# A conv, SiLU and ELU kernel on one core: block scales fetched and set earlier, taps moved between units, the last sums in one bank

## Chip, core and metric

One NeuronCore of a Trainium2 chip. The time is the device time of one execution in microseconds, the median of the runs shown. TensorE (PE; its weight loads are PEld), VectorE (DVE), ScalarE (ACT), GpSimd (POOL) and SyncE (SP, which issues most of the transfers) each work through a queue of their own in order.

## What is computed

```python
w = softmax(weight)                              # 8 heads x 7 taps
x = causal 7-tap convolution of x with w         # 8192 tokens x 192
h = x @ w_in;  x = (h * sigmoid(h)) @ w_out      # layer 0, SiLU, d_ff 2048
h = x @ w_in2; out = elu(h) @ w_out2             # layer 1, ELU, d_ff 2048
```

All in float32 accuracy. The kernel splits each factor into a high and a low part and multiplies high by high, high by low and low by high. From block 3 of layer 0 on, the low part of the activation g is float16, and to fit it is scaled by a power of two, one per block.

## The kernel before

The tokens stand in 16 blocks of 512, and a layer takes a block in 8 units, one for each eighth of d_ff (256 of 2048). Units are numbered in the order in which they run: blocks 0 and 1 of layer 0 share units 0 to 15, and block b from 2 on has units 8b to 8b+7, the first of which is called s. Layer 1 follows from unit 128.

From unit 20 on TensorE's queue holds for unit n: the in-products of n (18 matmuls, line 546, into a PSUM tile `h` with two buffers), then the out-products of an earlier unit. For blocks from 3 on these are the high products of unit n-3 (line 646), and after those of unit 8b+10 also the low products of block b: `low_c` (line 658) and `low_ab` (line 670), whose weights `w16` and activations `lo` are float16, in 64 x 64 tiles. So after block 5's low ab sums come the in-products of unit 51.

For unit n of a scaled block in layer 0, ScalarE makes SiLU in place in `h` (line 588) and the high part `g_hi` (line 580, scaled by `forth`), and VectorE the low part `lo` (line 583). `lo` is the last reader of `h`, so the in-products of unit n wait for `lo` of unit n-2.

Everything else is filled in by hand. `at(step, f, part)` notes f for a unit, and `run_fill(step)` issues what is noted for it ahead of that unit's SiLU, `g_hi` and `lo` on each queue (where a block ends, parts 1 and 2 go behind them). For the next block b this is, in order:

- the convolution: 14 taps on VectorE (line 499, 501), for the 128 rows of group 0 (512 tokens) and the folded 64 rows of group 1 in turn;
- `measure`: VectorE finds the largest magnitude of each row, and SP sends it to a small table in memory (`shared<-sum`, line 417, the share);
- `split_conv`: ScalarE and VectorE split the rows into high and low parts, and SP issues four crossings (`x_hl<-x_hl`, line 314) that bring each half of the rows to the other 64 partitions. Unit s reads crossed rows from its third pair of products on;
- `fetch`: SP brings the whole table to all partitions (`all<-shared`, line 421). It must wait for the share to land. The tile `all` has one buffer, for both layers' blocks and for the weights' bounds;
- `set_scale`: VectorE sums the table and makes `forth` and `back` (six small operations, lines 450 to 458).

In blocks 8 to 15 VectorE and ScalarE also make one eighth of layer 1's weights: the halves of `val` (lines 141, 145, 149) in units s-3 and s-2, then in unit s-1 three copies on ScalarE (lines 363, 211, 363). Layer 1's weight bound is measured up to unit 53, shared in 54, fetched by POOL in 56 and worked out by `finish_weight_scale(1)` in unit 58 (lines 473 to 443); unit 61 is the first to need it.

At the end `last_ab` sums the low ab products of the last block for two halves of 256 tokens. It has two PSUM banks for each half, one for the upper and one for the lower 64 rows of the contraction, and `add_ab` adds both to the output, one after the other, ahead of the store.

Of the kernel before, what the change touches and what calls it, by code (L numbers as in the profile page):

```python
# [9 lines left out]
F32 = mybir.dt.float32  # L10
# [14 lines left out]
P = 128  # L25
HP = 64
TB = 512
HT = TB // 2
# [10 lines left out]
NEW = 3  # L39
# [6 lines left out]
def kernel(  # L46
# [34 lines left out]
    ps_h = ctx.enter_context(tc.tile_pool(name="ps_h", bufs=2, space=bass.MemoryType.PSUM))  # L81
# [7 lines left out]
    ROWS = slice(0, HP), slice(HP, P)  # L89
# [219 lines left out]
    def load_x(b, *groups):  # L309
        for f in x_loads(b, *groups):  # L310
            f()
# [61 lines left out]
    def keep_ab(b, y):  # L373
        kept["ab", b] = tc.dram_tile([P, TB], F32, name="kept_ab")
        nc.sync.dma_start(out=kept["ab", b], in_=y)
# [25 lines left out]
    w16_t = {}  # L401
# [4 lines left out]
    def scaled(layer, b):  # L406
        return layer == 1 or b >= NEW

    def small(n=1, dtype=F32, tag=None):
        return scale_p.tile([P, n], dtype, tag=tag or f"small{n}", name=tag or "small")  # L410
# [8 lines left out]
    def fetch(key, queue=nc.sync):  # L419
        t = fixed.tile([P, 2 * P], F32, tag="all", name="all")  # L420
        queue.dma_start(out=t, in_=shared[key].to_broadcast([P, 2 * P]))
        shared[key] = t

    def measure(layer, b, *of):
        t = stat[layer, b] = small(2, tag="sum")
        for k, x in enumerate(of):
            nc.vector.tensor_reduce(
                out=t if len(of) == 1 else t[:, k : k + 1], in_=x, axis=AX.X, op=ALU.max, apply_absolute_value=True
            )
        share((layer, b), t)  # L430

    def power(out, of, exponent):

        nc.vector.tensor_scalar(
            out=of.bitcast(I32), in0=of.bitcast(I32), scalar1=EXP, scalar2=None, op0=ALU.bitwise_and
        )
        nc.vector.tensor_scalar(
            out=out.bitcast(I32), in0=of.bitcast(I32), scalar1=-1.0, scalar2=float((254 + exponent - 1) << 23),
            op0=ALU.mult, op1=ALU.add,
        )  # L440

    def inverse(out, of):
        nc.vector.tensor_scalar(
            out=out.bitcast(I32), in0=of.bitcast(I32), scalar1=-1.0, scalar2=float(254 << 23),
            op0=ALU.mult, op1=ALU.add,
        )

    def set_scale(layer, b):
        total = small(tag="total")
        nc.vector.tensor_reduce(out=total, in_=shared[layer, b], axis=AX.X, op=ALU.add)  # L450
        nc.vector.tensor_scalar(
            out=total, in0=total, scalar1=most[layer][:, 0:1], scalar2=TINY, op0=ALU.mult, op1=ALU.max
        )
        s = forth[layer, b] = small(tag="forth")
        power(s, total, 26)
        r = back[layer, b] = small(tag="back")
        inverse(r, s)
        nc.vector.tensor_tensor(out=r, in0=r, in1=down[layer], op=ALU.mult)
# [12 lines left out]
    def finish_weight_scale(layer):  # L471
        m = most[layer] = fixed.tile([P, 2], F32, tag=f"most{layer}", name="most")
        nc.vector.tensor_reduce(
            out=m, in_=shared[layer].rearrange("p (n two) -> p two n", two=2), axis=AX.X, op=ALU.max
        )
        largest = small(tag="total")
        nc.vector.tensor_scalar_max(largest, most[layer][:, 1:2], TINY)
        up[layer] = fixed.tile([P, 1], F32, tag=f"up{layer}", name="up")
        down[layer] = fixed.tile([P, 1], F32, tag=f"down{layer}", name="down")
        power(up[layer], largest, 14)  # L480
        inverse(down[layer], up[layer])
# [42 lines left out]
    g_t = {}  # L524
    g_of = {}
    acc_t = {}
# [133 lines left out]
                    rhs=g_t[u][1][ROWS[r], i, :], start=False, stop=last,  # L660
                )

    def low_ab(u, last, banks=None, tokens=slice(0, TB), first=False):

        layer, b, q = u
        for i in range(2):
            for j in range(2):
                for r in range(2):
                    bank = acc_t[layer, b, f"ab{r}"] if banks is None else banks[:, r, :]
                    nc.tensor.matmul(  # L670
                        out=bank[ROWS[j], :], lhsT=w16_t[layer, q][ROWS[r], i, ts(j, HP)],
                        rhs=g_t[u][1][ROWS[r], i, tokens], start=first and i == 0, stop=last and i == 1,
                    )

    def low_products(layer, b):
        us = [(layer, b, q) for q in range(NQ)]
        for u in us:
            low_c(u, u == us[-1])
        for u in us:
            low_ab(u, u == us[-1])  # L680

    def last_ab(tokens):

        bank = ps_h.tile([P, 2, TB], F32, tag="h", name="last")[:, :, 0:HT]
        for u in units[-NQ:]:
            low_ab(u, u == units[-1], bank, tokens, u == units[-NQ])
        return bank
# [67 lines left out]
    def end_steps(layer, b):  # L755

        both = xin.tile([P, TB], F32, tag="conv1", name="both")
        if layer == 0:
            y = mid.tile([P, TB], F32, tag="ab", name="mid_ab")
        else:  # L760
            y = xin.tile([P, TB], F32, tag="conv0", name="o")

        def plus(to, of):
            if scaled(layer, b):
                nc.vector.scalar_tensor_tensor(
                    out=to, in0=of, scalar=back[layer, b], in1=to, op0=ALU.mult, op1=ALU.add
                )
            else:
                nc.vector.tensor_add(out=to, in0=of, in1=to)

        def add(name, to):
            halves = [acc_t.pop((layer, b, f"{name}{r}")) for r in range(2)]
            scale = back[layer, b] if scaled(layer, b) else 1.0
            nc.scalar.activation(out=to, in_=halves[0], func=ACTF.Copy, scale=scale)  # L774
            plus(to, halves[1])

        def store_ab(cols=slice(0, TB)):
            nc.sync.dma_start(out=outT[0:P, b * TB + cols.start : b * TB + cols.stop], in_=y[:, cols])

        def add_ab(banks=()):  # L780
            if not banks:
                add("ab", y)
                if layer == 0:
                    keep_ab(b, y)
                elif b < NB - 1:
                    store_ab()
                return
            tokens, bank = banks
            for r in range(2):
                plus(y[:, tokens], bank[:, r, :])  # L790
            store_ab(tokens)

        return both, lambda: add("c", both), add_ab
# [24 lines left out]
    def at(step, f, part=0):  # L818
        fill.setdefault((max(step, 0), part), []).append(f)
# [5 lines left out]
    def spread(steps, first, n):  # L825
        for k, f in enumerate(steps):
            at(first + k * n // len(steps), f)
# [20 lines left out]
    for b in range(2, NB):  # L848
        s = where[0, b, 0]
        if b > 2:  # L850
            at(s - 14, lambda b=b: pending.extend(x_loads(b)) if b < 5 else load_x(b))
        steps = [f for fs in zip(*(conv_steps(b, g) for g in range(2))) for f in fs]
        found_it = [lambda b=b: measure(0, b, conv_t[b, 0], conv_t[b, 1])]
        splits = [lambda b=b, g=g: split_conv(b, g) for g in range(2)]
        if b <= 3:
            spread(steps + found_it * (b == NEW) + splits, s - 10, 7 if b > 2 else 8)
        elif b == 4:
            spread(steps, s - 10, 7)
            at(s - 4, found_it[0])
        else:  # L860
            for k, f in enumerate(steps):
                step = s - 8 if k < 1 else s - 7 if k < 2 else s - 6
                at(step, f, 0 if k < 5 else 1 if k < 10 else 2)
            at(s - 5, found_it[0])
        if b >= 4:
            for f in splits:
                at(s - 4 + (b == 4), f)
        if b >= NEW:
            at(s - 3 + (b == 4), lambda b=b: fetch((0, b)))
            at(s - 1, lambda b=b: set_scale(0, b))  # L870
    for b in range(NB):
        at(where[1, b, 0] - 9, lambda b=b: load_mid(b))
        at(where[1, b, 0] - 6, lambda b=b: split_mid(b), 1)
# [15 lines left out]
    look = where[0, 6, 6]  # L889
    at(look, lambda: set_weight_scale(1, found))  # L890
    at(look + 2, lambda: fetch(1, nc.gpsimd))
    at(look + 4, lambda: finish_weight_scale(1), 2)
    made = {}
    for k, q in enumerate([*range(1, NQ), 0]):
        s = where[0, 8 + k, 0]
# [9 lines left out]
    with tc.manual_schedule():  # L905
# [3 lines left out]
        for _ in range(9):  # L909
            nc.tensor.matmul(  # L910
                out=warm, lhsT=ones, rhs=ones.unsqueeze(1).to_broadcast([P, TB // P, P]), start=True, stop=True
# [82 lines left out]
        for rows, other, _ in PAIRS:  # L994
# [9 lines left out]
            out=conv_ps, in0=x_raw[1][:, 0, TAPS - 1 : TAPS - 1 + TB], scalar=tap_w[:, 0, TAPS - 1 : TAPS],  # L1004
# [80 lines left out]
        for s in range(4, TWO + 3):  # L1085
# [5 lines left out]
            q = s // 2 + 1  # L1091
# [24 lines left out]
        for s in range(TWO + 4, n_units):  # L1116
            u = units[s]
# [38 lines left out]
        banks = [(tokens, last_ab(tokens)) for tokens in HALF]  # L1156
# [49 lines left out]
```

## Time and profile before

| | |
|---|---|
| median of 3 runs | 1077.77 us (1077.63 to 1078.63) |
| the profiled execution | 1078.69 us, its span 1077.0 us |
| TensorE busy | 1068.6 us, 99% of the span |
| its weight loads | 840.8 us, 78% |
| VectorE, ScalarE | 820.3 us, 76%, and 813.4 us, 76% |
| GpSimd | 89.3 us, 8% |
| granted TensorE clock | 1.0 throughout |

The span runs from the first to the last instruction; all times of rows count from its start. A row of the timeline gives start, duration, engine, line, operation, output<-inputs, form and count, and in brackets how long the engine was idle before it and what ended that.

### The profile page before, as it was taken

Reading aid. Unit: us, or ns where it says so; the run is one execution under the profiler, and the core shown is the slowest. Engines: PE = TensorE matmul, PEld = TensorE weight load, DVE = VectorE, ACT = ScalarE, POOL = GpSimd, SP = SyncE. Lnnn points to the kernel's source line nnn. Section 1 sums busy time; section 2 is a strip of 40 time slices with the busy share of each in tenths; the row PEclk is TensorE's granted clock in tenths of the full one; section 3 lists DMA queues with packets and bytes.
Section 4 is the critical chain, followed back from the end, with each engine's and each line's share of the span. In section 5 each row is a group of like instructions: output and inputs, shape, how many; then the busy total and the mean of one; then the engine's idle time right before and its main releaser. Section 6 shows DMA issues by size and latency. Waiting matters only on the chain.

```text
span 1077.0 us, 25189 instructions
## 1 busy us (share of the span) xinstructions
PE 1068.6 (99%) x10755; PEld 840.8 (78%) x10755; DVE 820.3 (76%) x1125; ACT 813.4 (76%) x907; POOL 89.3 (8%) x139
## 2 busy tenths in 40 slices
PE   9999999999999999999999999999999999999998
PEld 6999978777777777787777787777777777877776
DVE  8998767777777888777567777778777777777766
ACT  7767766556677666676688988888988888888885
POOL 5521131000110011100200000000000000000000
PEclk9999999999999999999999999999999999999999
DMA  5413165323443332323541122212123210222200
GB/s 162 134 46 85 30 168 145 101 68 80 116 113 80 109 107 92 109 79 85 161 139 46 26 60 60 60 38 40 44 60 60 59 37 26 60 60 60 40 16 16
DMA packets 48768, 82.77 MB, mean 77 GB/s; under 512 B 10576, under 2 KB 22736, under 8 KB 48656
## 3 DMA queue, kind: packets, MB, share of 16 engines
q1 hardware_dynamic: 42416, 57.30, 21.5%
q0 software_dynamic: 6240, 23.86, 7.5%
q8 instruction: 84, 1.38, 0.6%
q14 instruction: 28, 0.23, 0.1%
HBM read 43.23 MB, written 18.12 MB: 57 GB/s over the span
## 4 chain that ended last, share of the span: by engine, by line
PE 94%; DVE 2%; DMA 2%; SPq 1%; issue 1%; ACT 1%; DVEq 0%
PE h L546 46%; PE ab L646 19%; PE c L646 9%; PE ab L670 9%; PE c L658 5%; PE ab L719 2%; PE c L719 1%; PE ab L627 1%; DMA x_hl<-x_hl 1%; DVE conv L501 1%; PE c L627 1%; SPq L314 0%; DMA all<-shared 0%; DVE lo L583 0%; DMA raw<-in_w_dram 0%
## 5 line engine op out<-in xcount | busy, mean ns | idle before, releaser
L546 PE MATMUL h<-x_hl,wi 64*128 64x512 f32 x4464 | 573.4, 388 | 3.2 <-DVE lo L583 2.3
L546 PEld LDWEIGHTS h<-x_hl,wi 64*128 64x128 f32 x4464 | 435.2, 184 | 96.9 <-issue 7.0
L592 DVE SCALAR_TENSOR_TENSOR g<-g,h 128x1024 f32<-128x1024 f32 x128 | 156.3, 1221 | 129.1 <-ACT g L591 129.1
L646 PE MATMUL ab<-g_hi,wo 64*128 64x512 f32 x1856 | 248.1, 386 | 0.0
L646 PEld LDWEIGHTS ab<-g_hi,wo 64*128 64x128 f32 x1856 | 173.9, 184 | 36.5
L583 DVE SCALAR_TENSOR_TENSOR lo<-h,forth,g_hi 128x1024 f16<-128x1024 f32 x104 | 133.4, 1282 | 83.8 <-ACT g_hi L580 83.7
L588 ACT ACTIVATE h<-h 128x1024 f32<-128x1024 f32 x104 | 104.8, 1008 | 92.8 <-PE h L546 90.6
L583 DVE SCALAR_TENSOR_TENSOR lo<-g,forth,g_hi 128x1024 f16<-128x1024 f32 x128 | 163.6, 1278 | 0.1
L590 ACT ACTIVATE g<-h 128x1024 f32<-128x1024 f32 x128 | 131.6, 1029 | 42.4 <-PE h L546 42.4
L580 ACT ACTIVATE g_hi<-g,forth 128x1024 fp32r<-128x1024 f32 x126 | 143.2, 1136 | 0.0
L646 PE MATMUL c<-g_hi,wo 64*128 64x512 f32 x928 | 143.0, 386 | 0.0
L591 ACT ACTIVATE g<-g 128x1024 f32<-128x1024 f32 x128 | 135.7, 1060 | 4.0
L580 ACT ACTIVATE g_hi<-h,forth 128x1024 fp32r<-128x1024 f32 x104 | 116.1, 1116 | 3.4
L670 PE MATMUL ab<-lo,w 64*64 64x512 f16 x1792 | 101.5, 376 | 0.0
L646 PEld LDWEIGHTS c<-g_hi,wo 64*128 64x128 f32 x928 | 86.9, 184 | 18.6 <-issue 0.4
L501 DVE SCALAR_TENSOR_TENSOR conv<-x_raw,tap_w,conv 128x512 f32<-128x512 f32 (+1 forms) x174 | 100.4, 631 | 0.2
L670 PEld LDWEIGHTS <-w 64*64 64x64 f16 x1920 | 55.9, 107 | 44.4
L658 PE MATMUL c<-lo,w 64*64 64x512 f16 x928 | 55.9, 379 | 0.0
L658 PEld LDWEIGHTS <-w 64*64 64x64 f16 x928 | 24.5, 106 | 27.7 <-issue 10.6
L573 ACT ACTIVATE g_hi<-h 128x1024 fp32r<-128x1024 f32 x22 | 22.5, 1023 | 23.4 <-PE h L546 23.4
L774 ACT ACTIVATE o<-ab,back 128x512 f32<-128x512 f32 x16 | 11.0, 687 | 32.1 <-PE ab L670 27.0
L719 PE MATMUL ab<-g_hi,wo 64*128 64x512 f32 x128 | 34.6, 387 | 0.0
(130 smaller groups left out, 813.5 us busy)
## 6 DMA issues: line engine op xcount, KB each, us to landing
x_hl<-x_hl SPq DMA_DIRECT2D x60, 256.0 KB, 3.8
raw<-in_w_dram POOLq DMA_DIRECT2D x16, 512.0 KB, 6.1
x_raw<-in_xT_dram SPq DMA_DIRECT2D x16, 259.0 KB, 4.1
kept_ab<-mid_ab SPq DMA_DIRECT2D x16, 256.0 KB, 2.0
raw<-in_w_dram POOLq DMA_DIRECT2D x32, 128.0 KB, 4.8
mid_ab<-kept_ab SPq DMA_DIRECT2D x16, 256.0 KB, 5.2
mid_c<-kept_c SPq DMA_DIRECT2D x32, 128.0 KB, 5.1
x_hl<-x_hl SPq DMA_DIRECT2D x30, 128.0 KB, 3.7
```

Of the source, the lines that this page charges most:

```text
L501: nc.vector.scalar_tensor_tensor(out=y, in0=x, scalar=w, in1=y, op0=ALU.mult, op1=ALU.add)
L546: nc.tensor.matmul(out=h[:, r, :], lhsT=w[ROWS[r], w_lo, ts(of, P)], rhs=x_part(layer, b, 3 * x_lo + part)[ROWS[r], :], start=n == 0, stop ...
L580: nc.scalar.activation(out=hi, in_=g, func=ACTF.Copy, scale=s)
L583: nc.vector.scalar_tensor_tensor(out=lo, in0=g, scalar=s, in1=hi.bitcast(F32), op0=ALU.mult, op1=ALU.subtract)
L588: return [lambda: nc.scalar.activation(out=g, in_=h, func=ACTF.Silu), high, low]
L590: lambda: nc.scalar.activation(out=g, in_=h, func=ACTF.Relu, scale=-1.0),
L591: lambda: nc.scalar.activation(out=g, in_=g, func=ACTF.Exp, scale=-1.0),
L592: lambda: nc.vector.scalar_tensor_tensor(out=g, in0=g, scalar=-1.0, in1=h, op0=ALU.add, op1=ALU.max),
L646: nc.tensor.matmul(out=acc_t[layer, b, f"{name}{r}"], lhsT=wo[ROWS[r], i, ts(k, P)], rhs=hi[ROWS[r], i, :], start=q == 0 and n in (0, 2), ...
L658: nc.tensor.matmul(out=acc_t[layer, b, f"c{r}"][ROWS[i], :], lhsT=w16_t[layer, q][ROWS[r], i, P:D], rhs=g_t[u][1][ROWS[r], i, :], start=Fa ...
L670: nc.tensor.matmul(out=bank[ROWS[j], :], lhsT=w16_t[layer, q][ROWS[r], i, ts(j, HP)], rhs=g_t[u][1][ROWS[r], i, tokens], start=first and i ...
L719: ins = nc.tensor.matmul(out=acc_t[0, b, name][0 : cols.stop - cols.start, :], lhsT=wo[ROWS[r], i, cols], rhs=g_t[0, b, q][part][ROWS[r], ...
```

## The change

- Block 4: its 14 taps, two a unit in units 22 to 28, go to units 22 (3), 23 (3), 24 (4), 25 (1), 26 (1) and 27 (2). Its measure goes from unit 28 to 27, its splits from 29 to 28, its fetch from 30 to 28 and its `set_scale` from 31 to 30.
- Blocks 5 to 15: the fetch goes from unit s-3 to s-4 and stands there ahead of the splits and their crossings; `set_scale` goes from s-1 to s-2. Block 3 keeps its units.
- `finish_weight_scale(1)` goes from the end of unit 58 to the beginning of unit 61.
- The last ab sums: each contraction over 128 rows is one matmul in a 128 x 64 tile and not two in 64 x 64 tiles, each half of the tokens has one bank, and one addition follows.

```diff
-    def low_ab(u, last, banks=None, tokens=slice(0, TB), first=False):
+    def low_ab(u, last, bank=None, tokens=slice(0, TB), first=False):
...
-                for r in range(2):
-                    bank = acc_t[layer, b, f"ab{r}"] if banks is None else banks[:, r, :]
+                for rows in ROWS if bank is None else (slice(0, P),):
+                    to = acc_t[layer, b, f"ab{rows.start // HP}"] if bank is None else bank
                     nc.tensor.matmul(
-                        out=bank[ROWS[j], :], lhsT=w16_t[layer, q][ROWS[r], i, ts(j, HP)],
-                        rhs=g_t[u][1][ROWS[r], i, tokens], start=first and i == 0, stop=last and i == 1,
+                        out=to[ROWS[j], :], lhsT=w16_t[layer, q][rows, i, ts(j, HP)],
+                        rhs=g_t[u][1][rows, i, tokens], start=first and i == 0, stop=last and i == 1,
                     )
...
-        bank = ps_h.tile([P, 2, TB], F32, tag="h", name="last")[:, :, 0:HT]
+        bank = ps_h.tile([P, 2, TB], F32, tag="h", name="last")[:, 0, 0:HT]
...
-            for r in range(2):
-                plus(y[:, tokens], bank[:, r, :])
+            plus(y[:, tokens], bank)
...
         elif b == 4:
-            spread(steps, s - 10, 7)
-            at(s - 4, found_it[0])
+            for k, f in enumerate(steps):
+                at((22, 22, 22, 23, 23, 23, 24, 24, 24, 24, 25, 26, 27, 27)[k], f)
+            at(s - 5, found_it[0])
...
+        if b >= NEW:
+            at(s - (3 if b == 3 else 4), lambda b=b: fetch((0, b)))
+            at(s - (1 if b == 3 else 2), lambda b=b: set_scale(0, b))
         if b >= 4:
             for f in splits:
-                at(s - 4 + (b == 4), f)
-        if b >= NEW:
-            at(s - 3 + (b == 4), lambda b=b: fetch((0, b)))
-            at(s - 1, lambda b=b: set_scale(0, b))
+                at(s - 4, f)
...
-    at(look + 4, lambda: finish_weight_scale(1), 2)
+    at(look + 7, lambda: finish_weight_scale(1))
```

## Rows read from the trace of the kernel before

**Rows 1.** The chain in order of time: blocks 4 to 7, low ab sums; start, length.
```profile
189.47 3.51 PE ab L670 x64
...
223.32 3.45 PE ab L670 x64
...
256.05 3.51 PE ab L670 x64
...
289.52 3.45 PE ab L670 x64
```
**Rows 2.** The timeline of all engines, 120 to 160 us.
```profile
126.32 1.12 ACT L580 ACTIVATE g_hi<-h,forth 128x1024 fp32r<-128x1024 f32 x1
...
128.04 1.27 DVE L583 SCALAR_TENSOR_TENSOR lo<-h,forth,g_hi 128x1024 f16<-128x1024 f32 x1
...
129.37 2.34 PE L546 MATMUL h<-x_hl,wi 64*128 64x512 f32 x18 [0.72 <-DVE lo L583]
...
145.11 0.42 DVE L450 TENSOR_REDUCE total<-all 128x1 f32<-128x256 f32 x1 [2.94 <-DMA all<-shared]
...
146.46 1.28 DVE L583 SCALAR_TENSOR_TENSOR lo<-h,forth,g_hi 128x1024 f16<-128x1024 f32 x1
...
147.80 2.33 PE L546 MATMUL h<-x_hl,wi 64*128 64x512 f32 x18 [1.13 <-DVE lo L583]
```
**Rows 3.** The timelines of TensorE and of GpSimd at block 6's first unit.
```profile
203.26 1.18 POOL L102 DMA_DIRECT2D raw<-in_w_dram  x2 [17.11 <-DVE found L238]
...
211.22 1.89 PE L546 MATMUL h<-x_hl,wi 64*128 64x512 f32 x14 [0.62 <-DMA x_hl<-x_hl]
```
**Rows 4.** The timeline of SP's queue: block 5's share and crossings, block 6's crossings.
```profile
165.37 0.33 SPq L417 DMA_DIRECT2D shared<-sum  x1
167.19 3.26 SPq L314 DMA_DIRECT2D x_hl<-x_hl  x4
...
199.92 4.87 SPq L314 DMA_DIRECT2D x_hl<-x_hl  x4
```
**Rows 5.** The timeline of all engines, 256 to 284 us.
```profile
263.65 0.40 DVE L473 TENSOR_REDUCE most<-all 128x2 f32<-128x256 f32 x1
...
264.72 1.00 DVE L427 TENSOR_REDUCE sum<-conv 128x1 f32<-128x512 f32 x2
...
266.98 2.34 PE L546 MATMUL h<-x_hl,wi 64*128 64x512 f32 x18 [0.45 <-DVE lo L583]
...
268.33 1.28 DVE L583 SCALAR_TENSOR_TENSOR lo<-h,forth,g_hi 128x1024 f16<-128x1024 f32 x1
```
**Rows 6.** The timeline of all engines, 336 to 352 us (block 10).
```profile
338.20 0.60 DVE L145 TENSOR_SCALAR val<-raw 128x768 uint16<-128x768 uint16 x1
...
338.83 0.96 DVE L149 SCALAR_TENSOR_TENSOR val<-mag,val 128x768 int32<-128x768 int32 x1
...
340.26 0.51 ACT L363 ACTIVATE wi<-val 128x384 fp32r<-128x384 f32 x1
...
342.76 2.20 PE L546 MATMUL h<-x_hl,wi 64*128 64x512 f32 x18
...
343.93 1.28 DVE L583 SCALAR_TENSOR_TENSOR lo<-h,forth,g_hi 128x1024 f16<-128x1024 f32 x1 [0.91 <-ACT g_hi L580]
...
346.16 2.20 PE L546 MATMUL h<-x_hl,wi 64*128 64x512 f32 x18
```
**Rows 7.** Line 417, the shares, 160 to 500 us: us from issue to landing.
```profile
DMA to landing us min/median/max: 2.8/3.0/4.5
```
**Rows 8.** Line 421, the fetches, 160 to 500 us: us from issue to landing.
```profile
DMA to landing us min/median/max: 3.5/4.0/6.8
```
**Rows 9.** The timelines of TensorE, weight loads and VectorE from 1062 us on.
```profile
1065.84 1.22 PEld L658 LDWEIGHTS <-w 64*64 64x64 f16 x28 [0.35 <-issue]
...
1069.31 3.66 PE L670 MATMUL last<-lo,w 64*64 64x256 f16 x128
...
1073.03 1.00 DVE L765 SCALAR_TENSOR_TENSOR o<-last,back,o 128x256 f32<-128x256 f32 x2 [0.15 <-PE last L670]
```

## Prediction

> **What bounds the kernel now.** I read the page first: TensorE is busy for nearly all of the span (its share stands in the table above), so only its few holes and its own work can give anything. The chain in order of time says where the holes are. The low ab sums of a block stand once in every block, 28 times from 156.74 to 1042.52 us, and their distance is a block's time. It is 32.73 us from block 5 to block 6, but 33.85 one block earlier and 33.47 one block later [rows 1]: 1.12 and 0.74 us over the even pace. All other distances are 32.73, save one over by 0.28 at 546 us, which the change doesn't touch. Before the first of these rows the timeline shows two holes that end with a `lo` of VectorE [rows 2], at 129.37 (unit 28) and 147.80 (unit 33). So the trace has four holes that this change can reach, and a tail.
>
> Each hole has its cause. An h tile has two buffers, so the in-products of unit n wait for `lo` of unit n-2. `lo` of 26 starts at 128.04 though its `g_hi` was ready at 127.44 [rows 2]: taps stood ahead of it. `lo` of 31 starts at 146.46 because `set_scale` of block 4 waited 2.94 us for its table [rows 2]. The hole at 211.22 (unit 48, block 6) waits 0.62 us for a crossing [rows 3]; the four crossings of this block took 4.87 us to issue, against 3.26 in block 5 [rows 4]. The hole at 266.98 (unit 61) waits for `lo` of 59, ahead of which layer 1's weight bound took 1.07 us (263.65 to 264.72) [rows 5].
>
> **The change part by part.** *Block 4.* With one tap in unit 25 and one in 26, `lo` of 26 is held by `g_hi` alone: 127.47 to 128.75, so unit 28 starts at 128.80 and not at 129.37. A start behind a wait costs 0.14 us more (the 18 in-products take 2.34 us there and 2.20 in the even pace) [rows 2, 6]. The taps moved to units 22 to 24 add one, one and two to what VectorE does there, 0.4 to 1.1 us a unit, in front of a `lo` that waits for ScalarE; at nothing, and 0.1 to 0.3 if that cover is thinner. The measure goes to unit 27 (about 1 us, like that of block 8 [rows 5]), so the share is out near 130.8. A share lands 2.8 to 4.5 us after its issue, median 3.0 [rows 7], and a fetch 3.5 to 6.8 us after its own, median 4.0 [rows 8]. So the table is there by about 138, just as unit 30 reaches `set_scale`, and unit 31 is free of it. Unit 33 then starts five units of 3.40 us (342.76 to 346.16 [rows 6]) after unit 28: 128.94 + 17.0 = 145.94. Today it starts at 147.80, with 0.14 behind it. **Gain 2.0 us.**
>
> *Block 6.* The fetch now stands ahead of the crossings on SP's queue and waits for the share to land. All four crossings and what SP issues behind them, the next x loads, wait with it (the taps that read those start about a block later). Take block 5: share at 165.37, landed at 168.4, fetch issued by 169.0, crossings from 169.0 instead of 167.19 and out by 172.3 instead of 170.45. Their reader, unit 40, starts at 177.25 (unit 80's 342.76 [rows 6] less five blocks of 32.73 and the two extras) and needs them 0.45 us later. With the 4 us that I allow for a landing (the middle of the fetch's row [rows 8], since the crossings' own doesn't stand here), 1.4 us remain. In block 6 a raw load of POOL starts at 203.26 [rows 3]. With its share as far ahead of the crossings' start of 199.92 as in block 5 [rows 4], so at 198.1, the crossings run from 201.7 to 205 and, with 4 to 5 us, land by 210; unit 48 needs them at 210.4. I take the full **1.12 us**; the bounds are 1.12 and, if the slow issue of 4.87 comes again or the raw load takes their turn, a loss of 1.
>
> *The weight bound out of unit 58.* `lo` of 59 comes 1.07 us sooner and the hole at unit 61 closes: **0.74 us**. But the fetched table has one buffer. Block 8's fetch is now in unit 60, and the weight bound reads its own table in unit 61 only. So SP, with block 8's crossings behind it, waits for that reduce. It stands behind `lo` of 60, which moves from 268.33 [rows 5] to about 267.4, held by its `g_hi`. The reduce ends near 269.05, the fetch lands 3.5 later at 272.55, and VectorE is there at 272.0. `set_scale` takes 1.35 us (145.11 to 146.46) [rows 2], then `val` 1.59 (0.60 and 0.96 and their starts) [rows 6], then `lo` of 62 ends at 276.7. Unit 64 could start at 266.36 + 3 x 3.40 = 276.56: 0.33 lost with the restart, and 0.35 more one unit on by the mechanism below. **Loss 0.7 us**, from 0.3 to 2 if the fetch takes 5.
>
> *Blocks 9 to 15, `set_scale` a unit sooner.* This puts it into unit s-2, in which VectorE also makes layer 1's weights. I follow block 10 [rows 6]. Today `val` is worked from 338.20 to 339.79 and ScalarE copies it at 340.26, the first of three copies ahead of unit 79's own two operations; `lo` of 79 runs from 343.93 to 345.21, and unit 81 starts at 346.16. With 1.35 us of `set_scale` ahead of `val`, `val` ends at 341.14, the copies start at 341.17, 0.91 later, and so does all behind them on ScalarE: `lo` of 79 ends at 346.12. TensorE starts 0.06 after (147.74 to 147.80) [rows 2], at 346.18, and pays the restart: 0.16 us in each of seven blocks, **a loss of 1.1 us**. From below it is nothing, if half a tenth is lost in my chain of starts; from above 0.3 a block, 2.1 in all. The table must be there at 338.2: share at 330.9, fetch at 333.95, landing 3.5 us later at 337.45. I take the lower end of the fetch's row because nothing stands ahead of it on the queue any more. There is 0.75 us to spare. Blocks 5 to 7 have no `val` there and lose nothing.
>
> *The last ab sums.* Today 128 sums of 256 tokens on 64 rows take 3.66 us, and VectorE's last two additions 1.00 [rows 9]. Afterwards there are 64 sums on all 128 rows, two at a time for four, so 32 rounds either way (a round of 512 tokens takes 0.216, since 64 sums by fours take 3.45 [rows 1], so one of 256 takes 0.108), and one addition of 0.50 at the end. There is one more change of tile shape, ahead of which the weight loads idle 0.35 us today [rows 9]; on the path I put it between nothing and 0.4 and take 0.25. **Gain 0.25 us.**
>
> The Trainium skill speaks against this edit: "TensorE: Matmul & The Clock Gate", Part 3, says that a weight load runs beside matmuls only where its row group differs, and with 128 rows none differs. In the trace two of the four tiles always share their rows, and 128 sums still take 3.66 us with their loads hidden, so the trace bears it out badly. By that rule the tail would be some 3 us longer, which is rival (c).
>
> **The sum.** 2.0 + 1.12 + 0.74 - 0.7 - 1.1 + 0.25 = 2.3 us less. The profiled execution took 1078.69 us, 1.69 more than its span of 1077.0, and becomes 1076.4; it lies 0.92 above the median of the runs, 1077.77, which becomes **1075.5 us**. About 0.2% (2.2 us) is what a measurement of this kernel can tell from no change, so the forecast sits on that edge.
>
> **The rivals.** (a) *The new waits don't show*, because ScalarE's chain keeps its slack in blocks 9 to 15 and block 8's fetch is quick. For it: the loss is 0.16 where starts are known to 0.05. The time is 1077.77 - 4.1 = 1073.7. (b) *The crossings come late* in blocks 5 and 6, where raw loads run beside them: the hole at 211.22 stays (1.12) and block 5 gets one of 0.5. For it: the slow issue of block 6; against it: the 1.4 us of room worked out above. 1077.1. (c) *Weight loads show in the last ab sums*: if each of the 32 rounds waits for a load as long as its sum, 0.108 us, the tail grows by 3.4 us: 1078.9. (d) *Slower: the fetch lands late in blocks 8 to 15.* The slack of 0.75 us goes first, then each further tenth costs VectorE, and TensorE, a tenth in eight blocks. It decides at a landing of 4.25 + 2.3/8, about 4.6 us; the 2.2 us more that I would call slower need 4.8. At 5.0, eight times 0.75 makes 6.0 us: 1081.5. For it: the fetch's row has a median of 4.0 and a largest of 6.8 [rows 8]; against it: those stood behind crossings. (e) *Block 4's holes stay*, moved to other units: 1077.5.
>
> **How the numbers follow.** Forecast 46%, (a) 22%, (b) 12%, (c) 7%, (d) 9%, (e) 4%. The forecast's own range is 1074.4 to 1076.6, some six tenths of it beyond the edge. So faster by over 0.2%: 0.28 and (a)'s 0.22, 0.50. Slower: (d), 0.09. Within: the rest, 0.41. The range goes from (a) with 0.3 us to spare, 1073.4, to (b) and the near part of (c), 1077.6.
>
> **What would show it.** In the profile after: no wait at unit 33, one of about 0.3 at unit 28; a distance of 32.73 us at block 6; for block 8 SP's fetch behind the weight bound's reduce; from block 9 to 15 distances of 32.9, each with a wait of one unit after the block's first; a tail with one addition of 0.5 us. Distances of 32.73 throughout would mean (a), holes that end with the table's transfer (d), holes that end with a crossing (b), and last ab sums over 5 us (c).

## The result, and the profile after

| | before | after |
|---|---|---|
| median of 6 runs each | 1077.92 us (1077.63 to 1078.63) | 1085.21 us (1083.73 to 1086.85) |
| the profiled execution, its span | 1078.69, 1077.0 us | 1085.7, 1084.0 us |

The ratio is 1.0063 (95% interval 1.0052 to 1.0073): the change made the kernel slower by 0.6%, where I forecast 1075.5 us and a range up to 1077.6. The kernel before beats it. Some executions of the kernel before, none of these six but 15 of the 95 beside the experiments, took 1082 to 1084 us at a mean granted clock of 0.996 to 0.998; the ratios count them, so medians are given too where that matters.

The chain in order of time for the changed kernel (start, length), as in [rows 1]:

```profile
155.50 3.45 PE ab L670 x64
190.18 3.45 PE ab L670 x64
227.25 3.45 PE ab L670 x64
260.36 3.45 PE ab L670 x64
293.36 3.45 PE ab L670 x64
...
558.92 3.45 PE ab L670 x64
```

The distances are 34.68, 37.07, 33.11 and 33.00 us for blocks 4 to 7. The eight blocks from 293.36 to 558.92 take 265.56, where eight even ones take 261.84 and the old extra at 546 us 0.28: 3.44 us are lost there. If the starts of the same unit's in-products are set side by side in both traces, the difference grows as follows (minus is a gain):

| stretch | forecast, us | measured, us |
|---|---|---|
| start and block 4 (units 28, 33, 34) | -2.0 | -1.24 |
| block 5's crossings (unit 40) | 0 | +1.96 |
| block 6's crossings (units 48, 49) | -1.12 | +3.20 |
| block 7's crossings (unit 56) | 0 | +0.34 |
| weight bound (units 61, 62) | -0.74 | -0.75 |
| block 8 | +0.7 | +0.27 |
| blocks 9 to 15 | +1.1 | +3.42 |
| layer 1 | 0 | +0.05 |
| last ab sums, to the end | -0.25 | -0.30 |
| sum | -2.3 | +6.95 |

The spans differ by 7.0. At unit 26, ahead of block 4's changed units, this trace was 0.13 us late already, so these units gained 1.37. Two places carry the miss: the crossings of blocks 5 to 7 (6.6 us from the forecast) and blocks 9 to 15 (2.3).

*Blocks 5 and 6.* The timelines of SP, GpSimd and TensorE of the changed kernel, answering to [rows 3, 4]:

```profile
164.13 0.33 SPq L417 DMA_DIRECT2D shared<-sum  x1
167.40 0.33 SPq L421 DMA_DIRECT2D all<-shared  x1
167.83 3.21 SPq L314 DMA_DIRECT2D x_hl<-x_hl  x4
...
169.29 1.18 POOL L102 DMA_DIRECT2D raw<-in_w_dram  x2 [17.13 <-DVE found L238]
...
178.29 1.89 PE L546 MATMUL h<-x_hl,wi 64*128 64x512 f32 x14 [1.66 <-DMA x_hl<-x_hl]
...
202.56 4.13 SPq L314 DMA_DIRECT2D x_hl<-x_hl  x4
...
203.97 1.18 POOL L102 DMA_DIRECT2D raw<-in_w_dram  x2 [17.11 <-DVE found L238]
...
213.72 2.34 PE L546 MATMUL h<-x_hl,wi 64*128 64x512 f32 x14 [2.41 <-DMA x_hl<-x_hl]
```

The fetch stands ahead of the crossings, waits 3.27 us for its share and lets them go 3.70 us after the share, 1.82 in [rows 4]. That much was forecast. But in the first unit of both blocks (40 and 48) TensorE now stands idle until a crossing lands: a hole of 1.66 and one of 2.41 us. A raw load (`raw<-in_w_dram`, three transfers by GpSimd that bring one of layer 1's weights, 768 KB) starts beside the crossings. The transfers of the changed kernel issued between 167.3 and 170.2 us (KB each, median us from issue to landing):

```profile
x_hl<-x_hl SPq DMA_DIRECT2D x2, 256.0 KB, 5.4
x_hl<-x_hl SPq DMA_DIRECT2D x2, 128.0 KB, 7.7
raw<-in_w_dram POOLq DMA_DIRECT2D x2, 128.0 KB, 5.9
all<-shared SPq DMA_DIRECT2D x1, 128.0 KB, 4.4
```

The same four crossings in the kernel before, issued between 167 and 170.4 us:

```profile
x_hl<-x_hl SPq DMA_DIRECT2D x2, 256.0 KB, 3.6
x_hl<-x_hl SPq DMA_DIRECT2D x2, 128.0 KB, 3.8
```

The last one took 3.7 us there and 8.3 now: issued at 169.97, it lands at 178.24, and TensorE starts at 178.29. At unit 48 a second cost is added. The windows of TensorE there (us, busy and count, granted clock, DMA share, GB/s):

```profile
208.00:212.00 4.00, 3.31 (x30) 1.00 1.03 256
212.00:216.00 4.00, 2.28 (x16) 0.87 0.52 111
216.00:220.00 4.00, 4.00 (x28) 0.71 0.01 4
```

The granted clock was 1.00 (2.4 GHz) before the hole of 2.41 us. The 0.87 and 0.71 behind it are means: in each microsecond from 215 to 218 the clock was 0.50 (1.2 GHz). The hole is 1.79 us longer than the old one, the unit 3.30: an estimate from these two gives about 1.5 us to the clock.

*Blocks 9 to 15.* The timeline of all engines in block 10 of the changed kernel, answering to [rows 6]:

```profile
338.21 0.33 SPq L421 DMA_DIRECT2D all<-shared  x1
...
342.78 0.42 DVE L450 TENSOR_REDUCE total<-all 128x1 f32<-128x256 f32 x1 [0.45 <-DMA all<-shared]
...
344.76 0.96 DVE L149 SCALAR_TENSOR_TENSOR val<-mag,val 128x768 int32<-128x768 int32 x1
...
345.75 0.53 ACT L363 ACTIVATE wi<-val 128x384 fp32r<-128x384 f32 x1 [1.34 <-DVE val L149]
...
349.44 1.28 DVE L583 SCALAR_TENSOR_TENSOR lo<-h,forth,g_hi 128x1024 f16<-128x1024 f32 x1 [2.52 <-ACT g_hi L580]
...
350.77 1.43 PE L546 MATMUL h<-x_hl,wi 64*128 64x512 f32 x10
```

The table landed 4.5 us after its issue, VectorE waited 0.45 for it, and `val`, the copies and `lo` of 79 follow late, in the order that was forecast. Unit 81 is 0.40 us later than the pace, unit 80 0.16 and unit 82 0.15.

*Block 4 and the tail.* The timeline of all engines around block 4's first units, answering to [rows 2]:

```profile
127.71 1.28 DVE L583 SCALAR_TENSOR_TENSOR lo<-h,forth,g_hi 128x1024 f16<-128x1024 f32 x1 [0.42 <-ACT g_hi L580]
...
129.05 1.91 PEld L546 LDWEIGHTS h<-x_hl,wi 64*128 64x128 f32 x18 [0.56 <-DVE lo L583]
...
143.59 1.89 PE L546 MATMUL h<-x_hl,wi 64*128 64x512 f32 x14 [0.19 <-DMA x_hl<-x_hl]
...
146.68 2.20 PE L546 MATMUL h<-x_hl,wi 64*128 64x512 f32 x18
```

`lo` of 26 waits for ScalarE alone, but 0.24 us later than I took (0.13 of this is the late start of the trace). The forecast for unit 33, 145.94, missed that and a wait of block 4's own crossings at unit 32, which makes the unit 3.90 us long. The tail of the changed kernel, answering to [rows 9]:

```profile
1076.70 3.42 PEld L670 LDWEIGHTS <-w 128*64 128x64 f16 x64 [0.23 <-issue]
1076.71 3.68 PE L670 MATMUL last<-lo,w 128*64 128x256 f16 x64
...
1080.43 0.48 DVE L765 SCALAR_TENSOR_TENSOR o<-last,back,o 128x256 f32<-128x256 f32 x1 [0.45 <-PE last L670]
```

64 loads of 128 rows run beside their sums: 3.68 us, where 128 half sums took 3.66.

### The profile page after: what moved, and what is told of

It is laid out like the page before. It is cut to its first block, busy times and chain, and to the rows that moved or that the text cites. A ratio compares the mean times of both kernels' runs of the same rounds, so it can differ in the third digit from the quotient of the medians.

```text
span 1084.0 us, 25051 instructions
## 1 busy us (share of the span) xinstructions
PE 1074.1 (99%) x10691; PEld 832.1 (77%) x10691; DVE 819.2 (76%) x1123; ACT 814.9 (75%) x907; POOL 89.5 (8%) x139
## 4 chain that ended last, share of the span: by engine, by line
PE 89%; DMA 5%; DVE 2%; ACT 2%; issue 1%; SPq 0%; POOL 0%; DVEq 0%; POOLq 0%
PE h L546 43%; PE ab L646 17%; PE ab L670 9%; PE c L646 8%; PE c L658 5%; DMA x_hl<-x_hl 3%; PE ab L719 2%; PE c L719 1%; DMA all<-shared 1%; PE ab L627 1%; DMA shared<-sum 1%; PE c L627 1%; DVE lo L583 1%; ACT g_hi L580 1%; SPq L314 0%
## 5 line engine op out<-in xcount | busy, mean ns | idle before, releaser
L670 PEld LDWEIGHTS <-w 64*64 64x64 f16 (+1 forms) x1856 | 55.8, 107 | 44.5 <-issue 0.2
L658 PEld LDWEIGHTS <-w 64*64 64x64 f16 x928 | 24.5, 106 | 27.7 <-issue 10.6
```

The source lines that it names most:

```text
L658: nc.tensor.matmul(out=acc_t[layer, b, f"c{r}"][ROWS[i], :], lhsT=w16_t[layer, q][ROWS[r], i, P:D], rhs=g_t[u][1][ROWS[r], i, :], start=Fa ...
L670: nc.tensor.matmul(out=to[ROWS[j], :], lhsT=w16_t[layer, q][rows, i, ts(j, HP)], rhs=g_t[u][1][rows, i, tokens], start=first and i == 0, s ...
```

## The experiments

Ratios are to the kernel before, on the same chip, with 95% intervals. Losses at units are against the starts of the kernel before, as in the table above.

**e1: fetch and `set_scale` of blocks 5 to 15 as before.**

```diff
+        if b in (3, 4):
+            at(s - b, lambda b=b: fetch((0, b)))
         if b >= NEW:
-            at(s - (3 if b == 3 else 4), lambda b=b: fetch((0, b)))
-            at(s - (1 if b == 3 else 2), lambda b=b: set_scale(0, b))
+            at(s - (2 if b == 4 else 1), lambda b=b: set_scale(0, b))
...
+        if b >= 5:
+            at(s - 3, lambda b=b: fetch((0, b)))
```

> The changed kernel, but in blocks 5 to 15 fetch and set_scale stand where they stood before (units s-3 and s-1). Theory A (the whole loss comes from moving these two in blocks 5 to 15; the other three parts gain what the two traces show, 1.25 at block 4, 0.75 at the weight bound, 0.3 at the end): 2.3 us faster than before, 1075.6 us, ratio 0.998, with block 6's old hole of 1.1 us still there. Rival (block 4's own moves already push SP's transfers of blocks 5 and 6 back): the holes at units 40 and 48 stay in part, 1079 us or more.

0.9977 (0.9968 to 0.9986). The trace has -1.64 us at block 4, -0.75 at units 61 and 62, 0.3 less from the last ab sums on, and nothing else of size. So the whole loss is in these two moves.

**e2: only `set_scale` back in unit s-1.**

```diff
-            at(s - (1 if b == 3 else 2), lambda b=b: set_scale(0, b))
+            at(s - (2 if b == 4 else 1), lambda b=b: set_scale(0, b))
```

> The changed kernel with only set_scale of blocks 5 to 15 back in unit s-1; the fetch stays ahead of the crossings. Theory A (in blocks 5 to 7 it is the fetch's place on SP's queue that costs, 5.6 us; in blocks 8 to 15 mostly set_scale ahead of val and its wait for the table, 3.7 us, of which about 1 is crossings): holes at units 40 and 48 stay, blocks 8 to 15 come back to 32.73 us save one or two, 1085.2 - 2.7 = 1082.5 us. Rival (VectorE's earlier set_scale holds everything up, the crossings too): all holes go, 1075 to 1077 us.

1.0014 (1.0002 to 1.0027). Blocks 8 to 15 lose 0.37 (block 12) and 0.77 (block 15) and nothing else, as expected. The holes were smaller than expected: none at unit 40, 1.11 us at unit 48, 0.53 at unit 56. Block 5's crossings were issued at 167.22, 0.61 sooner than in the changed kernel's profile, and the last two landed in 6.8 and 6.5 us. The traced execution took 1078.58 us, where the median of the ten is 1080.01, so others can have had larger holes.

**e3: the raw loads beside the crossings of blocks 5 and 6 later.**

```diff
-    looks = [(b, *n) for b in range(3, 6) for n in ((6, 9), (7, 13), (8, 14))][:NQ]
+    looks = [(b, *n) for b in range(3, 6) for n in ((6, 9), (8, 16 - 3 * (b == 5)), (8, 14))][:NQ]
```

> The changed kernel, but two of layer 1's weights are looked at later, so that POOL's raw loads that wait for their buffer start after units 40 and 48 and no longer beside the crossings of blocks 5 and 6. Theory A (the crossings lose their turn to the raw loads): crossings land 4 us after the issue as before, both holes go, the distances of the low ab sums of blocks 4 to 6 come near 33, 5 us less: 1080 us or a little under. Rival (it is enough that the crossings are issued 1.5 to 2 us later; the raw loads do no harm): the holes stay at 1.7 and 2.4 us, 1085 us.

0.9996 (0.9987 to 1.0004). The raw loads were issued at 174.74 and 206.83 us, where the changed kernel had 169.29 and 203.97: behind the issue of the crossings, though not behind units 40 and 48, which start 1 to 2 us later. No hole at units 40 and 48; block 6's old one is gone too. Block 7 still loses 0.35, blocks 8 to 15 together 2.7. The transfers of e3 issued from 167 to 170.4 us:

```profile
x_hl<-x_hl SPq DMA_DIRECT2D x2, 256.0 KB, 5.9
x_hl<-x_hl SPq DMA_DIRECT2D x2, 128.0 KB, 6.3
all<-shared SPq DMA_DIRECT2D x1, 128.0 KB, 4.9
```

The first raw load came 1.4 us before the last crossing landed. Without it these crossings still take 6.3 us, not 3.8, nor the 4 that I expected: behind the fetch they take 2.5 longer. The x loads that follow don't explain it: they were issued from 171.01 on, when the first crossing (167.66) would have landed by the 3.3 us of the kernel before, but it took 5.65. With the raw load as well the last one takes 8.3 in the changed kernel's first profile, but 6.5 in e2 and 7.0 in e12, so the raw load's part is 0.2 to 2. In block 10 of e3 the table is in time, and the wait is the mechanism that I forecast, alone:

```profile
336.07 0.42 DVE L450 TENSOR_REDUCE total<-all 128x1 f32<-128x256 f32 x1
...
344.07 2.35 PE L546 MATMUL h<-x_hl,wi 64*128 64x512 f32 x18
347.62 2.20 PE L546 MATMUL h<-x_hl,wi 64*128 64x512 f32 x18
```

It costs 0.16 at unit 81 and 0.15 more at unit 82.

**e4: `val` ahead of `set_scale` in unit s-2.**

```diff
-            at(s - (1 if b == 3 else 2), lambda b=b: set_scale(0, b))
+            if b < 8:
+                at(s - (1 if b == 3 else 2), lambda b=b: set_scale(0, b))
...
             at(s + step, lambda q=q, i=i: made[q][i](), 2 * (step == 2))
+        at(s - 2, lambda b=8 + k: set_scale(0, b))
```

> The changed kernel, but in unit s-2 of blocks 8 to 15 val is worked ahead of set_scale. Theory A (the loss there is ScalarE's copies of val, which start later by set_scale and by its wait for the table): copies start as before, waits of 0.2 to 0.6 at unit s+1 and s go but for those on crossings, 1.5 to 2.6 us less: 1082.6 to 1083.7. Rival (VectorE simply has 1.35 us too much in this unit, whatever comes first): the same 1085.2.

1.0019 (1.0006 to 1.0032). Blocks 8 to 15 lose 0.33 (block 12) and 0.63 (block 15), both for crossings, instead of 3.7. Block 10 of e4:

```profile
339.02 0.96 DVE L149 SCALAR_TENSOR_TENSOR val<-mag,val 128x768 int32<-128x768 int32 x1
...
339.90 0.41 DVE L450 TENSOR_REDUCE total<-all 128x1 f32<-128x256 f32 x1
...
340.46 0.51 ACT L363 ACTIVATE wi<-val 128x384 fp32r<-128x384 f32 x1
...
346.36 2.20 PE L546 MATMUL h<-x_hl,wi 64*128 64x512 f32 x18
```

VectorE does the same work in this unit, so the rival falls: it is the order. The copies start right behind `val` again, and the work on `val` covers the table's flight.

**e5: the diffs of e3 and e4 together.**

> The changed kernel with the raw loads after units 40 and 48 (as in e3) and val ahead of set_scale (as in e4); fetch and set_scale stay sooner, fetch ahead of the crossings. Theory A (the change lost by these two collisions and by nothing else of size): holes at units 40, 48 and behind the first units of blocks 8 to 15 go; what stays is a wait of 0.3 us for the crossings of block 12 and of 0.6 in block 15. e3's ratio 0.9996 less 2.2 us: 0.9975 of the kernel before. Rival (each of the two edits only moved the loss, and together they don't add): 0.999 or more.

0.9964 (0.9951 to 0.9977), by medians 1076.13 to 1078.91 us, 0.9974: the change as it is, with its two collisions out of the way, beats the kernel before. Its trace (1077.81 us) keeps 0.61 at block 7, 0.21 at block 12 and 1.19 at block 15, all for crossings.

**e6: the diffs of e1 and e3 together.**

> The kernel before with block 4's edits, the weight bound's and the last sums', fetch and set_scale of blocks 5 to 15 as before, and the raw loads after units 40 and 48. Theory A: the same as e1 without block 6's old hole of 1.1 us, every distance of the low ab sums of blocks 4 to 15 at 32.73 us: 0.9977 less 0.001, 0.9967 of the kernel before. Rival (the raw loads, set later, meet the crossings of block 7 or the weight bound instead): 0.998 or more, with a wait at unit 56 or 61.

0.9956 (0.9939 to 0.9973), by medians 1075.14 to 1078.91 us, 0.9965; its trace is 3.5 us shorter than that of the kernel before, 0.33%. The chain of e6:

```profile
155.37 3.45 PE ab L670 x64
188.09 3.45 PE ab L670 x64
...
286.27 3.45 PE ab L670 x64
```

Every block takes 32.73 us. This is the fastest version here by median, though its interval overlaps e5's.

**e7: the kernel before, raw loads a unit sooner.**

```diff
-    looks = [(b, *n) for b in range(3, 6) for n in ((6, 9), (7, 13), (8, 14))][:NQ]
+    looks = [(b, *n) for b in range(3, 6) for n in ((6, 9), (7, 13 - (b < 5)), (8, 14))][:NQ]
```

> The kernel before, with nothing of the change, but two of layer 1's weights are looked at one unit sooner, so that the raw loads start some 3.4 us sooner and run beside the crossings of blocks 5 and 6, which are issued when they were. Theory A (a crossing beside a raw load is slow, whoever was late): a hole of 1 to 2.5 us at unit 40, where before has none, and one of 2 to 3 us at unit 48, where before has 0.6; 2 to 4 us slower than before, ratio 1.002 to 1.004. Rival (it needs crossings that are issued later; the transfers share without harm): ratio 1.000, no hole at unit 40.

1.0001 (0.9982 to 1.0021). The trace (1077.49 us, where the median is 1078.45) has no hole at unit 40, and block 6's old one is gone: theory A fell. The raw loads were issued 1.45 us sooner (169.08, 201.80), not 3.4. The transfers of e7 issued from 198 to 208 us:

```profile
x_hl<-x_hl SPq DMA_DIRECT2D x2, 256.0 KB, 6.9
raw<-in_w_dram POOLq DMA_DIRECT2D x1, 512.0 KB, 4.9
...
x_hl<-x_hl SPq DMA_DIRECT2D x2, 128.0 KB, 5.7
```

A crossing beside a raw load is slow here too, one of the first two took 8.5 us. But the raw load is out sooner, and the last crossing, issued at 204.38, lands at 210.0, in time. So in this execution slowness alone makes no hole. The holes that the traces show have crossings whose room was used up already: by the fetch's wait and its transfer, or, in block 6 of the kernel before, by a slow issue [rows 4].

**e8: e4 with the fetch behind the crossings, still in unit s-4.**

```diff
-        if b >= NEW:
-            at(s - (3 if b == 3 else 4), lambda b=b: fetch((0, b)))
+        if b in (3, 4):
+            at(s - b, lambda b=b: fetch((0, b)))
...
         if b >= 4:
             for f in splits:
                 at(s - 4, f)
+        if b >= 5:
+            at(s - 4, lambda b=b: fetch((0, b)))
```

> e4's kernel (val ahead of set_scale), but in blocks 5 to 15 the fetch stands behind the crossings in the same unit; the raw loads stay where they are. Theory A (the fetch's place on SP's queue is what makes the crossings late): no hole at unit 40, block 6 and block 7 as before (1.1 us and none over pace), no wait for crossings in blocks 12 and 15. The table comes some 2 to 3 us later, and set_scale, which now stands behind val, waits for it by up to 0.5 us in blocks 8 to 15: between 0.9977 and 1.0005 of before. Rival (the crossings are late for another reason): holes at units 40 and 48 as in e4, 1.002.

1.0091 (1.0065 to 1.0117), the slowest of all. The crossings were on time, as theory A says (block 5's landed in 3.3 to 3.9 us again); the table was not. The timelines of SP, VectorE and TensorE of e8 in block 6:

```profile
205.51 0.55 SPq L421 DMA_DIRECT2D all<-shared  x1
...
212.23 0.42 DVE L450 TENSOR_REDUCE total<-all 128x1 f32<-128x256 f32 x1 [6.46 <-DMA all<-shared]
...
215.81 4.21 PE L546 MATMUL h<-x_hl,wi 64*128 64x512 f32 x18 [5.39 <-DVE lo L583]
```

I had priced this wait at 0.5 us, in blocks 8 to 15. In blocks 5 to 7 there is no `val` to cover it, and the fetch itself takes 6.7 us beside the raw load. So a `set_scale` in unit s-2 needs the fetch ahead of the crossings, and that makes the crossings late: the two moves hang together.

**e9, e10, e11: one part alone on the kernel before** (block 4's; the weight bound's; the last sums', each as in the diff of the change).

> The kernel before with block 4's edits alone. Theory A (they gain what the changed kernel shows there, 1.25 us, 1.64 where no crossing is late): 0.9988 to 0.9985 of before; unit 28 0.3 to 0.5 sooner, unit 33 1.1 to 1.5. As I forecast it: 2.0 us, 0.9981, unit 33 1.86 sooner. Rival (the taps in units 22 to 24 hold VectorE up there): unit 24 or 25 later than before, under 1 us gained.

> The kernel before with the weight bound moved to unit 61 alone; block 8's fetch stays in unit 61. Theory A: 0.75 us less, 0.9993, the hole at unit 61 gone. Rival (the bound in unit 61 now holds back block 8's fetch, which stands in the same unit, and its table comes late to set_scale in unit 63): the 0.75 gained at unit 61 is given back at unit 65, 1.000.

> The kernel before with the last ab sums alone in 128-row tiles, one bank and one addition. One look, for the trace: the last 64 sums in 3.66 to 3.70 us as their 128 halves before (by the rule of rival (c), 7 us), a single addition of 0.50 behind them, the end 0.3 us sooner than before.

e9: 0.9989 (0.9979 to 0.9998); -1.05 us at unit 34, though this trace was 0.32 late at unit 26, so the units 28, 33 and 34 gained 1.38. e10: 0.9993 (0.9979 to 1.0007); -0.75 at units 61 and 62, and none of it given back at unit 65. By time alone that is not told from no change; the trace tells it. Yet unit 33 of e10, which that edit doesn't touch, came 0.91 us sooner than in [rows 2], since block 4's table landed sooner. So single traces of block 4 differ by most of a microsecond of themselves. e11, one run, taken for its trace: the last sums took 3.68 us and one addition 0.48; from the last block of c sums (1065.88, [rows 9] 1065.84) to the end of the last addition it is 7.77 us, before 8.19.

**e12: the changed kernel again, unaltered, on another chip.**

> The changed kernel as it is, a second time, because e2 and e4, which alter nothing of it ahead of block 5's crossings on SP's queue, had smaller holes at units 40 and 48 (0 and 1.1, 0.9 and 1.6 us) than its first profile (1.7 and 2.4). Theory A (the holes are a race of two transfers, whose size goes from run to run and chip to chip with some tenths of the share's landing): between 1.0035 and 1.0065 of before, with other holes than in the first profile. Rival (these holes are fixed by the changed kernel's own order): 1.0063 again, holes of 1.7 and 2.4 us.

1.0034 (1.0019 to 1.0049). Blocks 5 to 7 lost 0.33, 0.61 and 0.69 us in this trace, 1.6 together and not 5.5; its granted clock was 1.0 throughout. Blocks 8 to 15 lost 3.6, about as much as the first time. So the loss in blocks 8 to 15 came again, and that in blocks 5 to 7 differs from execution to execution: in block 5 the share took 0.36 less to land here, the crossings left at 167.40, 0.43 sooner, and the last of them landed in 7.0 us and not 8.3. Each trace is one draw: this execution took 1081.55 us, where the median is 1083.10, and the first one 1085.7, where it is 1085.21.

## Why the prediction was wrong

*The step that failed* is in "Block 6": "With the 4 us that I allow for a landing (the middle of the fetch's row [rows 8], since the crossings' own doesn't stand here), 1.4 us remain." The issue times behind it held: the crossings left 3.70 us after the share, where I had 3.6. The landing did not. For the last crossing of block 5 it is 3.7 us by itself, 3.7 again with the fetch issued behind it (e8), 6.3 behind the fetch (e3), and 6.5 to 8.3 with the raw load as well (e2, e12, the first profile). My 4 us were counted from the end of the issue; so counted, that crossing took 2.6 us before and 7.2 after. I counted what the fetch does to SP's queue, its wait, and not that its own transfer lengthens the landing of those that follow at once. In blocks 8 to 15 too, with no raw load beside them as they land, the crossings' 128 KB take 5.8 us in e5 and 3.8 in the kernel before (medians). Rival (b) named the place; its price (0.5 and the old 1.12) was worked out with the same 4 us, and neither it nor the forecast had a term for crossings in blocks 7, 12 and 15.

The trace of the kernel before held a warning: a landing for block 6 could be read from it. The last crossing there, issued at 204.10 beside a raw load and with no fetch ahead:

```profile
x_hl<-x_hl SPq DMA_DIRECT2D x1, 128.0 KB, 7.1
```

The Trainium skill, "DMA: Bandwidth & Descriptors", section "Issuing engines are not separate DMA queues", says that transfers issued by several engines run on the same 16 DMA engines and interleave, so that another queue saves issue time only. The 7.1 and 8.3 us beside GpSimd's load agree; the 6.3 is behind a transfer of the same queue.

*Block 6's gain of 1.12* was wrongly assigned: issuing the fetch first doesn't close that hole, moving the raw load does (e3, e6, and e7's trace).

*Blocks 9 to 15* had the right mechanism, shown by e4, and two wrong sizes. The late `lo` costs two units and not one, 0.31 us a block (e3), near my upper bound of 0.3. And the table's landing, which I took as 3.5 us, is 4.5 with the crossings right behind it, so that VectorE waits 0.32 to 0.45 for it in four of the seven blocks (0.12 to 0.53 in six of them in e12); this is the beginning of rival (d), whose bound of 4.25 + 2.3/8 is 4.54 and not 4.6. With blocks 12 and 15, whose crossings cost 0.2 to 1.2 in e4 and e5, these make up the 3.4.

*Block 8* lost 0.27, not 0.7: the fetch behind the weight bound's reduce landed in time. *The weight bound* (0.75) and *the last sums* (0.30) came as worked out. Rival (c) fell, and with it, for this shape, the rule behind it: "TensorE: Matmul & The Clock Gate", Part 3, of the Trainium skill lets a weight load run beside matmuls only where the row group differs, but 64 loads of 128 rows took 3.42 us beside sums of 3.68, with none to spare for waiting in turn.

*Block 4* gained 1.24 of 2.0, or 1.37 without the trace's late start. Two terms were left out: `g_hi` of 26 came 0.24 later (0.13 of it that start), and the block's own crossings, behind the fetch now, hold unit 32, which takes 0.50 more.

What stays open is why the share lands 2.8 us after its issue in one trace and 3.3 in another; in e12 the sooner share goes with a loss of 0.3% in place of 0.6, but the chip was another one too. And why the fetch lengthens the crossings' landing, by its bytes, by its one row of memory that all partitions read, or otherwise, was not tried.

## What to carry to other kernels

A transfer that is moved ahead of others on a queue can cost them twice: the wait in front of it, and a longer landing while it is itself under way; so allow for the followers a landing that was measured beside such a neighbour, not the median of a quiet stretch. Work that hides a table's flight (`val` here) belongs ahead of the instruction that waits for the table, and whatever a sooner instruction on one engine feeds on another (ScalarE's copies) is to be followed for two units, not one. When a change of many parts turns out slower, put its parts back singly: here three of four were worth 0.23%, and with two loads moved 0.44% (0.19 and 0.35 by medians).

## What the runs showed of the hardware

- Behind a 128 KB fetch that one row of memory feeds to all partitions, 0.4 us ahead on the same queue, the last copies took 6.3 us to land and not 3.8 (e3, block 5). In block 6 of e3 the second to fourth copy left 2.8 us or more behind the fetch and took 3.9 to 4.1. With a 768 KB load from another queue beside them a copy took 7.1 without the fetch ahead (block 6 before) and as much as 8.3 with it.
- TensorE's granted clock fell from 1.00 to 0.50 (1.2 GHz) behind a hole of 2.41 us, and in e8 with a hole of 5.39 (210.42 to 215.81); the windows there:

```profile
212.00:216.00 4.00, 0.19 (x2) 0.64 0.05 16
216.00:220.00 4.00, 4.00 (x20) 0.50 0.00 0
220.00:224.00 4.00, 4.00 (x39) 1.00 0.01 4
```

  20 matmuls were done in 4 us there against 39 in the next 4. After e4's hole of 1.62 us it stayed at 1.00.
- Where two transfers meet, moving the one either way can free the other: block 6's hole of 0.62 us went with the raw loads 1.45 us sooner (e7's trace) and with them some 2 us later (e6).
- In the kernel before a crossing's issue took 2.7, 3.4 and 3.0 us (at 200.61, 300.67 and 464.30) where the others take 0.6 to 1.5; in each case a packet of the instruction queue (q8) had started 0.04 to 0.33 us before. The two go together in the trace; which causes which was not tried. The first of these used up the room of block 6's crossings.
